# Second forward transform stage as 64x32 matmul tiles, with forward shuffles from 64 partitions to eight on two DMA queues

## The chip, the cores and the metric

One core of a Trainium2 chip runs the whole kernel. The metric is the device time in microseconds of one execution; the profile's times are microseconds from the start of its span. TensorE (PE) does the matmuls, VectorE (DVE) and ScalarE (ACT) read the results out of PSUM ("evacuation"), GpSimd (POOL) does small work and issues DMAs, SyncE (SP) issues DMAs only.

## The reference

A long convolution per channel, gated, and then an MLP over the tokens. S = 2048 tokens, D = 448 channels, F = 1792; everything that matters is this:

```python
x = A_q
h  = x + A(layernorm(x), A_k, A_v, A_shift_k, A_ssm_k, A_ssm_D)
h2 = h + B(layernorm(h), B_w1, B_b1, B_w2, B_b2)

def A(q, k, v, shift_k, ssm_k, ssm_D):
    kv = causal_shift_conv(k, shift_k) * v          # 4 taps, per channel
    y  = irfft(rfft(pad(kv, 2 * S)) * rfft(pad(ssm_k, 2 * S)))[:S]
    return q * (y + kv * ssm_D)

def B(x, w1, b1, w2, b2):                            # over the tokens
    u = gelu(einsum("bsd,sf->bdf", layernorm(x), w1) + b1)
    return transpose(einsum("bdf,fs->bds", u, w2) + b2)
```

## The kernel before

The transforms are matmuls with tables of sines that the kernel builds itself. Tokens are split as 128 partitions times R = 16, so a forward transform has two stages. The same two stages run for the filter (tag "k", source `KT`, target `TK`) and for kv (tag "u", source `V`, target `TU`).

First stage, `emit_stage1` (matmul at L1040): 128x32 tiles, four of them side by side in the columns of the array, so that 8 matmuls fill one pair of PSUM banks, 128 x 896 values. One evacuation (L1050, or L1048 where the term with `ssm_D` is added for the filter, which only DVE does) writes the pair into a buffer in SBUF. A group is four such pairs (`jh` 0 to 3); there are four groups for k and four for u, so 16 evacuations each. After `jh` 1 and after `jh` 3, half of the group's buffer is moved by three DMAs (L1056): partitions 0 to 31 and 96 to 127 by POOL, 32 rows to 8 partitions each, and 32 to 95 by SP, 64 rows to 16 partitions. Each names the columns of `TK` or `TU` that it writes, which is half of them.

Second stage, `emit_stage2` (matmul at L1075): 8 pairs `jj`, and in each pair two PSUM buffers `h`. Each buffer takes four matmuls with 128 rows and 64 columns of the block table `FW`, and is evacuated (through `evac`, L719 and L720 on ACT, L722 and L723 on DVE) over the input in `TK` or `TU`.

Then `emit_products_i1` multiplies the two spectra on DVE (L1108, 16 products), runs the first inverse stage in 64x128 tiles (L1120), evacuates, and shuffles back by POOL and SP DMAs (L1144, and L1133 for the last pair) to 8 partitions each. The second inverse stage `emit_i2` (L1240) combines, normalizes and feeds `emit_mlp` (L1365, L1375, L1387). Ahead of all this `emit_kT` transposes the filter (L1019), and `emit_kv` transposes k (L947), makes the short convolution by matmuls with 64 rows (L973), and multiplies by v on DVE (L988).

Nothing of this order is fixed in the code. `_Sched` collects all operations with their dependences, and a list scheduler places them on the engines: an engine that is free takes the ready operation with the lowest rank. The ranks are the numbers in `WHEN`, one for each step of a tag in the order in which the steps are emitted; `WHERE` says for operations that may run on ACT or DVE whether they go to ACT ("a"), to DVE ("d") or to whichever the scheduler finds ("f"). Buffers come from pools: `psum` has 8 banks, taken in pairs by the transform stages; `gring` holds the first stage's group buffers.

`emit_tables` builds `FW` for the second stage, and `MA`, `MB` and `MN` for the first inverse stage, from a per-partition index (`pc`, bit fields) and iotas on POOL.

Of the kernel before, what the change touches and what calls it, by code (L numbers as in the profile page):

```python
# [7 lines left out]
ALU = mybir.AluOpType  # L8
# [4 lines left out]
    "dummy": (283,),  # L13
    "tables": (138, 234, 288, 20, 81, 325, 139, 217,),
    "loads": (91, 107, 134, 143, 231, 216, 80, 297, 0, 238, 183, 285, 228, 299, 145,),
    "kv": (290, 148, 151, 174, 63, 282, 100, 192, 205, 47, 18, 112, 141, 45, 207, 160, 233,),
    "kT": (201, 13, 14, 175, 200, 130, 54, 53,),
    "k1": (132, 135, 152, 226, 122, 144, 165, 213, 68, 51, 154, 167, 89, 168, 262, 336,),
    "k2": (23, 150, 83, 97, 224, 227, 140, 153, 258, 248, 180, 195, 169, 219, 338, 235,),
    "u1": (71, 86, 116, 123, 46, 82, 176, 221, 117, 215, 261, 316, 173, 184, 277, 278,),  # L20
    "xload": (156, 298, 314, 302,),
    "bias": (75, 171,),
    "q": (271, 208, 318, 93, 268, 185, 279, 280, 264,),
    "u2": (133, 142, 220, 210, 241, 249, 64, 114, 159, 196, 137, 189, 1, 115, 252, 251,),
    "i1": (179, 121, 99, 3, 190, 96, 186, 149, 188, 240, 203, 202, 128, 92, 212, 95,),
    "ct": (36, 187, 87, 300,),
    "xn": (257, 17, 6, 222, 161, 317,),
    "w1a": (329, 239, 230, 55,),
    "w1b": (306,),
    "warm": (291, 307, 265, 27, 292, 147, 330, 320, 5, 304, 270, 38, 19, 315, 284, 62, 333, 327, 105, 118, 191, 295,  # L30
        324, 259, 56, 8, 332, 113, 236, 273, 206, 198, 182, 274,),
    "i2": (260, 69, 103, 39, 15, 31, 293, 28, 108, 242, 90, 84, 88, 331, 22, 197, 204, 33, 110, 237, 164, 323, 256,
        310, 73, 214, 223, 170, 44, 79, 157, 177, 16, 211, 328, 281, 131, 250, 4, 247, 158, 294, 109, 40, 29, 104,
        34, 243, 267, 129, 98, 287, 70, 178, 67, 162, 246, 120, 155, 2, 125, 11, 229, 42, 253, 272, 59, 124, 119,
        266, 12, 78, 194, 276, 127, 41, 313, 10, 102, 61, 255, 21, 37, 66, 24, 232, 199, 321, 312, 76, 308, 296, 52,
        111, 303, 163, 319, 58, 65, 339, 209, 26, 326, 337, 289, 85,),
    "w2": (146,),
    "mlp": (218, 57, 136, 126, 77, 30, 25, 48, 60, 9, 305, 72, 166, 245, 301, 172, 50, 181, 418, 419, 420, 421, 422,
# [3 lines left out]
    "kv": "ddaffffa",  # L42
    "kT": "fadfdddd",
    "k1": "fafaafaffaff",
    "k2": "dfdffadaafdafada",
    "u1": "fffaafadaaddafaa",
    "bias": "a",
    "u2": "fdaafafaaaaadafa",
    "i1": "affadfaaffdaffaf",
    "ct": "ffda",  # L50
    "xn": "aaff",
    "i2": "aaffaadafddf",
# [518 lines left out]
def _build(nc, A_q, A_k, A_v, A_shift_k, A_ssm_k, A_ssm_D, B_w1, B_b1, B_w2, B_b2, out):  # L571
# [5 lines left out]
    Bsz, S, D = A_q.shape  # L577
# [48 lines left out]
    with ctx:  # L626
# [47 lines left out]
        o_GR = (o_WR, o_WR + 8 * DB, o_X, o_X + 8 * DB)  # L674

        def GR_(s):
            return view(o_GR[s], [R // 4, 2, D])
# [13 lines left out]
        gring = _Pool(4)  # L691
# [36 lines left out]
        def emit_tables():  # L728
# [6 lines left out]
            o_p = small(80)  # L735
            frow = view(o_fr, [128], i32)
            srow = view(o_s, [16], i32)
            pc = view(o_p, [12], i32)
            pcf = view(o_p + 48, [6], f32)
# [33 lines left out]
            op("pool", lambda e, W: e.iota(pc[:, 0:1], [[0, 1]], base=0, channel_multiplier=128), w=[(o_p, 4)])  # L773
            op("pool", lambda e, W: e.iota(gcol, [[0, 8], [512, 16]], base=0, channel_multiplier=0), w=[(o_gc, 512)],
               n=128, est=190.0)
            op("pool", lambda e, W: e.iota(chi, [[0, 2], [1, 4], [0, 16]], base=0, channel_multiplier=0),
               w=[(o_gc + 512, 512)], n=128, est=190.0)
            for a, b_, c_ in ((0, 112, 14), (112, 128, 2)):
# [3 lines left out]
                op("pool", lambda e, W, a=a, b_=b_, c_=c_: e.iota(chm[:, a:b_], [[0, 2], [1, 4], [0, c_]], base=0,  # L782
                                                                 channel_multiplier=0),
                   w=[(o_gc + 2048 + 4 * NB, 512, "cm")], n=128, est=190.0)
            for k, (b0, st_) in enumerate(((2048, -2048), (2048, 2048), (0, 2048))):
                for a, b_ in (((0, 128),) if k == 0 else ((0, 112), (112, 128))):
                    op("pool", lambda e, W, k=k, b0=b0, st_=st_, a=a, b_=b_: e.iota(
                        cph[:, 128 * k + a:128 * k + b_], [[st_, 2], [0, (b_ - a) // 2]], base=b0, channel_multiplier=0),
                       w=[(o_gc + 1536 + 512 * k, 512, "cp%d" % k)], n=128, est=190.0)
# [7 lines left out]
            fields = ((5, 12), (0, 2048), (9, 3), (7, 15), (7, 15), (11, 3), (13, 1), (11, 2))  # L797
            o_fd = small(64)
            fd = view(o_fd, [16], i32)
            for i, (sh, mk) in enumerate(fields):  # L800
                op("pool", lambda e, W, i=i, sh=sh: e.memset(fd[:, i:i + 1], sh), w=[(o_fd + 4 * i, 4)], est=34.0)
                op("pool", lambda e, W, i=i, mk=mk: e.memset(fd[:, 8 + i:9 + i], mk), w=[(o_fd + 32 + 4 * i, 4)], est=34.0)
            op("dve", lambda e, W: e.tensor_tensor(out=pc[:, 4:12], in0=pc[:, 0:1].broadcast_to([128, 8]), in1=fd[:, 0:8],
                                                   op=ALU.logical_shift_right),
               r=[(o_p, 4), (o_fd, 32)], w=[(o_p + 16, 32)], n=8)
            op("dve", lambda e, W: e.tensor_tensor(out=pc[:, 4:12], in0=pc[:, 4:12], in1=fd[:, 8:16], op=ALU.bitwise_and),
               r=[(o_p + 16, 32), (o_fd + 32, 32)], w=[(o_p + 16, 32)], n=8)
            for i in (10, 11):
                op("dve", lambda e, W, i=i: e.tensor_tensor(out=pc[:, 4:5], in0=pc[:, 4:5], in1=pc[:, i:i + 1],
                                                            op=ALU.bitwise_or),  # L810
# [639 lines left out]
```

## Time and profile before

| | before |
|---|---|
| median of 3 runs | 178.2 us (177.69 to 178.92) |
| profiled execution: its own time, its span | 178.13 us, 175.9 us |
| PE, DVE, ACT, POOL busy | 166.1, 102.0, 92.2, 63.3 us |
| second stage matmuls (L1075) | 128, 15.8 us busy |
| first stage matmuls (L1040) | 256, 15.3 us busy |
| first inverse stage matmuls (L1120) | 128, 14.0 us busy |
| forward shuffles (L1056), POOL | 32 of 112 KB, median 3.8 us to landing |
| forward shuffles (L1056), SP | 16 of 224 KB, median 3.7 us to landing |
| inverse shuffles (L1144), POOL | 14 of 196 KB, median 4.6 us to landing |

A group of instructions is read as line, engine, operation, output from input, shapes, count, then busy time and mean duration of one, then the idle time of its engine just before and what ended it. A duration of a matmul is its latency; matmuls overlap, so busy time is less than count times duration. The chain of waits is followed back from the last instruction, at each step to what released it.

### The profile page before, as it was taken

To read this page: it belongs to the slowest core of one execution; us is meant where nothing else is said; L and a number is where in the kernel's file an instruction comes from. 1 tells how busy PE (TensorE), PEld (TensorE's weight loads), DVE (VectorE), ACT (ScalarE), POOL (GpSimd) and SP (SyncE) were. 2 spreads that over 40 slices of the span, in tenths; PEclk is the share of its full clock that TensorE was granted. 3 is DMA by queue.
4 is the path that set the end of the run, shared out by engine and by line. 5 is a ranking of instruction groups with operands and counts; after the bars stand their busy time and mean duration, and the time that the engine had idled before them with its cause. 6 is when DMAs were issued, how large, how long until landed. Compare 5 with 4: busy or idle time off the path is not lost.

```text
span 175.9 us, 3619 instructions
## 1 busy us (share of the span) xinstructions
PE 166.1 (94%) x1445; PEld 95.6 (54%) x1445; DVE 102.0 (58%) x189; ACT 92.2 (52%) x131; POOL 63.3 (36%) x157
## 2 busy tenths in 40 slices
PE   6999999879979999998999999999999999999994
PEld 2786745342323333644544455555557777777784
DVE  6995696848999999998998860000001231331331
ACT  3799958888979999966982656412120000000000
POOL 8576628670600643894888760000000000000000
PEclk9999999999999999999999999999999999999999
DMA  5999855992849386569999999910000111011111
GB/s 174 416 334 332 268 165 201 325 352 71 250 98 383 110 214 198 167 179 390 383 396 405 421 419 417 419 77 0 0 4 0 52 52 52 16 40 52 52 52 52
DMA packets 15444, 35.13 MB, mean 200 GB/s; under 512 B 3820, under 2 KB 9484, under 8 KB 15428
## 3 DMA queue, kind: packets, MB, share of 16 engines
q1 hardware_dynamic: 12164, 28.00, 43.4%
q0 software_dynamic: 3072, 6.80, 12.6%
q8 instruction: 11, 0.18, 0.4%
q10 hardware_dynamic: 192, 0.11, 0.2%
q14 instruction: 5, 0.04, 0.1%
HBM read 22.05 MB, written 1.84 MB: 136 GB/s over the span
## 4 chain that ended last, share of the span: by engine, by line
PE 68%; ACT 10%; POOL 7%; DMA 7%; DVE 4%; issue 2%; DVEq 0%; POOLq 0%
PE ps L1387 24%; PE ps L1375 12%; PE ps L1365 9%; ACT arena L719 8%; DMA arena<-arena 7%; PE ps L1040 4%; PE ps L1006 3%; POOL arena L1056 3%; PE ps L947 3%; PE ps L1240 3%; PE ps L1075 2%; PE ps L1019 2%; PE ps L973 2%; PE ps L1120 2%; DVE arena L1259 1%
## 5 line engine op out<-in xcount | busy, mean ns | idle before, releaser
L1390 DVE SCALAR_TENSOR_TENSOR arena<-ps,arena 128x448 bf16<-128x448 f32 (+2 forms) x17 | 11.1, 656 | 57.4 <-PE ps L1387 57.4
L1387 PE MATMUL ps<-arena 128*128 128x448 bf16 (+2 forms) x238 | 42.7, 342 | 0.0
L1387 PEld LDWEIGHTS ps<-arena 128*128 128x128 bf16 x238 | 33.3, 145 | 9.5
L719 ACT CAST arena<-ps 128x896 bf16<-128x896 f32 (+1 forms) x29 | 23.4, 948 | 1.2 <-PE ps L1075 1.1
L1365 PE MATMUL ps<-arena 128*128 128x448 bf16 x112 | 22.9, 353 | 0.4 <-DVE arena L1318 0.4
L1056 POOL DMA_DIRECT2D arena<-arena x32 | 17.5, 553 | 14.1 <-ACT arena L1050 12.9
L1050 ACT CAST arena<-ps 128x896 bf16<-128x896 f32 x24 | 20.3, 919 | 3.8 <-PE ps L1040 3.5
L1375 PE MATMUL ps<-arena 128*128 128x448 bf16 x112 | 21.8, 353 | 0.0
L1075 PE MATMUL ps<-arena 128*64 128x448 bf16 x128 | 15.8, 360 | 3.4 <-DMA arena<-arena 1.8
L1355 ACT ACTIVATE arena<-ps,arena 128x448 bf16<-128x448 f32 x14 | 8.6, 633 | 19.4 <-PE ps L1375 17.7
L1108 DVE TENSOR_TENSOR arena<-arena 128x1792 bf16<-128x1792 bf16 x16 | 16.7, 1080 | 0.2
L1365 PEld LDWEIGHTS ps<-arena 128*128 128x128 bf16 x112 | 10.6, 98 | 11.5 <-DVE arena L1318 2.5
L1375 PEld LDWEIGHTS ps<-arena 128*128 128x128 bf16 x112 | 10.9, 98 | 10.2
L1040 PE MATMUL ps<-arena 128*32 128x448 bf16 x256 | 15.3, 356 | 0.4 <-DVE arena L988 0.3
L1120 PE MATMUL ps<-arena 64*128 64x448 bf16 x128 | 14.0, 352 | 1.0 <-ACT arena L719 0.9
L1144 POOL DMA_DIRECT2D arena<-arena x14 | 8.2, 588 | 17.4 <-ACT arena L719 16.6
L1075 PEld LDWEIGHTS ps<-arena 128*64 128x64 f16 x128 | 5.7, 108 | 12.8 <-ACT arena L719 3.6
L1287 ACT ACTIVATE arena<-arena 128x448 bf16<-128x448 f32 x14 | 8.0, 575 | 5.9 <-DVE arena L1259 5.7
L988 DVE TENSOR_TENSOR arena<-ps,arena 128x512 bf16<-128x512 f32 (+1 forms) x16 | 9.0, 617 | 2.7 <-PE ps L973 2.7
L1120 PEld LDWEIGHTS ps<-arena 64*128 64x128 f16 x128 | 5.1, 94 | 9.5 <-ACT arena L719 5.0
L719 ACT COPY arena<-ps 128x1024 bf16<-128x1024 bf16 (+1 forms) x9 | 8.9, 1019 | 0.9 <-PE ps L1154 0.6
L1040 PEld LDWEIGHTS ps<-arena 128*32 128x32 f16 x256 | 5.1, 95 | 7.8 <-DVE arena L988 1.9
(94 smaller groups left out, 207.0 us busy)
## 6 DMA issues: line engine op xcount, KB each, us to landing
arena<-in_B_w_dram SPq DMA_DIRECT2D x8, 896.0 KB, 12.0
arena<-in_B_w_dram SPq DMA_DIRECT2D x2, 2048.0 KB, 17.1
arena<-arena SPq DMA_DIRECT2D x16, 224.0 KB, 3.7
arena<-arena POOLq DMA_DIRECT2D x32, 112.0 KB, 3.8
arena<-in_B_w_dram SPq DMA_DIRECT2D x2, 1536.0 KB, 18.7
arena<-arena POOLq DMA_DIRECT2D x14, 196.0 KB, 4.6
arena<-in_A_k_dram SPq DMA_DIRECT2D x4, 448.0 KB, 5.7
arena<-in_A_v_dram SPq DMA_DIRECT2D x4, 448.0 KB, 9.0
```

Source lines behind the costliest of these rows:

```text
L719: return e.copy(out=dst(), in_=src())
L988: return e.tensor_tensor(out=v, in0=u.rearrange("p t (r d) -> p t r d", d=64), in1=v, op=ALU.mult)
L1040: op("pe", lambda e, W, b=b, r=r, q=q, x=x, c0=c0: e.matmul(PS[32 * q:32 * q + 32, b.slots[x], 0:D], E[:, 2 * r + x, c0:c0 + 32], src[:, r ...
L1050: return e.copy(out=dst, in_=Ppair(b)) if W == "act" else e.tensor_copy(out=dst, in_=Ppair(b))
L1056: shuf[tag].append(op(q_, lambda e, W, g=g, i=i, a=a, nu=nu, jh=jh: e.dma_start(T[a + i:a + i + 4 * nu - 3:4].rearrange("p (j k) c d -> p ...
L1075: op("pe", lambda e, W, b=bs[h], h=h, j=j, c=c, par=par: e.matmul(PS[64 * par:64 * par + 64, b.slots[c], 0:D], FW[:, 64 * c:64 * c + 64], ...
L1108: op("dve", lambda e, W, m=m, i=i: e.tensor_tensor(out=MR(m.slots[0]).rearrange("p (x y) d -> p x y d", x=2), in0=TU[:, i].unsqueeze(2).br ...
L1120: k = op("pe", lambda e, W, b=bs[h], m=ms[h], par=par, t=t, tab=tab, xy=xy, P=P: e.matmul(Pb(b, par), tab[P, :], MR(m.slots[0])[P, xy, :], ...
L1365: op("pe", lambda e, W, r=r, fc=fc, b=bs[fc]: e.matmul(Pb(b), W1A[:, r, 128 * fc:128 * fc + 128], Q[:, r, :], start=(r == 0), stop=(r == R ...
L1375: op("pe", lambda e, W, r=r, fc=fc, b=b: e.matmul(Pb(b), W1B[:, r, 128 * (fc - n0):128 * (fc - n0) + 128], Q[:, r, :], start=(r == 0), sto ...
L1387: op("pe", lambda e, W, r=r, fc=fc, b=b, d0=d0, d1=d1: e.matmul(Pb(b)[:, d0:d1], W2[fc // 7][:, fc % 7, r:S:R], G[:, fc, d0:d1], start=(fc ...
L1390: op("dve", lambda e, W, r=r, b=b, A=A, d0=d0, d1=d1: e.scalar_tensor_tensor(out=X[:, r, d0:d1], in0=Pb(b)[:, d0:d1], scalar=bm[:, r:r + 1 ...
```

## The change

The second stage's matmuls become 64x32 tiles: 16 in each pair `jj`, which cover both buffers `h`, with the two row halves of the array and its four column strips used in turn (`tile_position`). The columns are paired as `jj` and `jj + 8` in place of `2 jj` and `2 jj + 1`; products, first inverse stage and inverse shuffles follow this pairing.

The first stage's groups are halved: eight groups of two pairs for k and eight for u, with the four 32-column tiles of one pair taken from two rows `r` in place of four. Eight buffers of half the size hold them. When a group is complete, two DMAs move it, rows 0 to 63 by POOL and rows 64 to 127 by SP, each to 8 partitions, 224 KB; for the upper half the target's two blocks of 32 partitions are exchanged. Each names all of `TK` or `TU` as its target.

The tables change to match (one more bit field, an exclusive or, other iota patterns), the row with `ssm_D` is loaded twice, and `WHEN` and `WHERE` hold new numbers for all tags ahead of the MLP's last matmuls.

```diff
 WHEN = {
...
-    "kv": (290, 148, 151, 174, 63, 282, 100, 192, 205, 47, 18, 112, 141, 45, 207, 160, 233,),
+    "kv": (133, 102, 131, 266, 43, 156, 243, 35, 101, 150, 178, 236, 261, 245, 244, 210, 230,),
...
-    "k1": (132, 135, 152, 226, 122, 144, 165, 213, 68, 51, 154, 167, 89, 168, 262, 336,),
-    "k2": (23, 150, 83, 97, 224, 227, 140, 153, 258, 248, 180, 195, 169, 219, 338, 235,),
-    "u1": (71, 86, 116, 123, 46, 82, 176, 221, 117, 215, 261, 316, 173, 184, 277, 278,),
+    "k1": (145, 213, 62, 134, 116, 139, 68, 198, 99, 158, 0, 160, 183, 196, 231, 246,),
+    "k2": (40, 27, 212, 26, 93, 137, 141, 185, 163, 215, 57, 138, 220, 79, 305, 6,),
+    "u1": (228, 254, 197, 232, 47, 238, 182, 250, 45, 87, 49, 154, 168, 284, 95, 214,),
...
-    "u2": (133, 142, 220, 210, 241, 249, 64, 114, 159, 196, 137, 189, 1, 115, 252, 251,),
-    "i1": (179, 121, 99, 3, 190, 96, 186, 149, 188, 240, 203, 202, 128, 92, 212, 95,),
+    "u2": (37, 5, 157, 165, 132, 294, 179, 201, 151, 34, 162, 277, 229, 82, 268, 314,),
+    "i1": (226, 56, 108, 105, 135, 115, 64, 202, 65, 58, 199, 200, 28, 83, 123, 143,),
...
-        o_GR = (o_WR, o_WR + 8 * DB, o_X, o_X + 8 * DB)
+        o_GR = tuple(o + 4 * DB * s for o in (o_WR, o_X) for s in range(4))
...
-        gring = _Pool(4)
+        gring = _Pool(8)
...
-            fields = ((5, 12), (0, 2048), (9, 3), (7, 15), (7, 15), (11, 3), (13, 1), (11, 2))
+            fields = ((7, 6), (0, 2048), (10, 1), (8, 15), (8, 15), (12, 3), (12, 1), (10, 8), (11, 8))
...
-            for i in range(R // 4):
+            for i in range(R // 2):
                 g = _Buf(gring)
-                for jh in range(4):
+                pi = 32 * (i >> 2) + (i & 3)
+                for jh in range(2):
...
-                    if jh % 2 == 0:
-                        continue
-                    for q_, a, nu in (("pool", 0, 8), ("pool", 96, 8), ("sp", 32, 16)):
-                        shuf[tag].append(op(q_, lambda e, W, g=g, i=i, a=a, nu=nu, jh=jh: e.dma_start(
...
-                           br=[g], w=[(o_T + (4 * j + jh - 1) * 2 * DB, 4 * DB, tag) for j in range(4)],
-                           dmab=4 * nu * 4 * DB, keng=nu, rate=350.0))
+                for t in range(2):
+                    p0 = 64 * t + (pi ^ 32 * t)
+                    shuf[tag].append(op("sp" if t else "pool", lambda e, W, g=g, p0=p0, t=t: e.dma_start(
+                        T[p0:p0 + 29:4].rearrange("p (j k) c d -> p j (k c d)", k=2),
+                        GR_(g.slots[0])[64 * t:64 * t + 64].rearrange("p k c d -> p (k c d)")),
+                       br=[g], w=[(o_T, 32 * DB, tag)], dmab=64 * 4 * DB, keng=8, rate=350.0))
...
-                for h in range(2):
-                    sch.t0 = (T_K2 if scale else T_U2) + T_D2 * (2 * jj + h)
-                    for c in range(2):
-                        for par in range(2):
-                            j = 2 * jj + par
-                            op("pe", lambda e, W, b=bs[h], h=h, j=j, c=c, par=par: e.matmul(
-                                PS[64 * par:64 * par + 64, b.slots[c], 0:D], FW[:, 64 * c:64 * c + 64], T[:, j, h, :],
-                                start=True, stop=True),
+                for c in range(2):
+                    sch.t0 = (T_K2 if scale else T_U2) + T_D2 * (2 * jj + c)
+                    for h in range(2):
+                        for F_ in range(2):
+                            for t in range(2):
+                                j = jj + 8 * F_
+                                g0 = 64 * (t ^ h) + 32 * F_
+                                P = slice(64 * t, 64 * t + 64)
+                                op("pe", lambda e, W, b=bs[h], h=h, j=j, c=c, g0=g0, P=P, t=t: e.matmul(
+                                    PS[g0:g0 + 32, b.slots[c], 0:D], FW[P, 32 * c:32 * c + 32], T[P, j, h, :],
+                                    start=True, stop=True, tile_position=(64 * t, g0)),
...
```

## The prediction

> **What bounds the kernel now.** I read the page first, then busy time by stretch, then the chain of waits, then the timeline around the two places where a forward stage hands its data to the next. The page gives the frame:
>
> ```profile
> span 175.9 us, 3619 instructions
> PE 166.1 (94%) x1445; PEld 95.6 (54%) x1445; DVE 102.0 (58%) x189; ACT 92.2 (52%) x131; POOL 63.3 (36%) x157
> PE 68%; ACT 10%; POOL 7%; DMA 7%; DVE 4%; issue 2%; DVEq 0%; POOLq 0%
> ```
>
> A busy share of 94% for TensorE is an average over very different stretches, and TensorE's ends are modelled. The stretches tell more (start and end, length, then busy time and number of instructions for PE, PEld, DVE, ACT, POOL):
>
> ```profile
> 18.00:36.00 18.00, 16.29 (x358) 9.11 (x356) 14.10 (x21) 14.53 (x18) 10.60 (x21) 1.00 0.75 244
> 36.00:52.00 16.00, 14.74 (x168) 5.97 (x168) 13.30 (x14) 13.41 (x17) 5.67 (x11) 1.00 0.59 188
> 52.00:73.00 21.00, 19.16 (x186) 7.63 (x184) 20.59 (x27) 20.73 (x26) 8.24 (x15) 1.00 0.68 212
> 92.00:175.90 83.90, 81.01 (x439) 52.34 (x437) 21.37 (x44) 14.97 (x30) 10.63 (x27) 1.00 0.35 137
> ```
>
> From 92 us on it is the MLP's matmuls, which the change doesn't touch. From 52 to 73 us (second stage of u, products, first inverse stage) DVE and ACT are both busy 98 to 99% of the time: nothing that TensorE does faster shows there. From 36 to 52 us DVE is idle for 16.00 - 13.30 = 2.70 us and ACT for 2.59 us, some 2.6 us each. The number of evacuations is the same after the change (16 a stage, 896 columns each), so 2.6 us is the most that this stretch can give back. The clock column is 1.00 throughout, so clock plays no part.
>
> The chain of waits shows what that idle time is made of (start, length, what):
>
> ```profile
> 28.25 1.53 POOL arena L1056 x3
> 29.85 1.03 POOL arena L1056 x2
> 30.93 4.97 DMA arena<-arena
> 35.99 0.96 PE ps L1075 x8
> 37.95 0.95 PE ps L1075 x8
> 39.67 0.97 PE ps L1075 x8
> ...
> 45.70 1.07 POOL arena L1056 x2
> 46.77 4.02 DMA arena<-arena
> 50.83 0.99 PE ps L1075 x8
> ```
>
> Twice it runs through forward shuffles: POOL issues them (L1056), they land, and only then does the second stage (L1075) run, for k at 35.99 and for u at 50.83. The matmuls of the second stage stand in it too, four times for about 0.96 us and, at 63.42, once for 0.51.
>
> **The change, part by part.** All sums are against the profiled execution: span 175.9, its own time 178.13 us, that is 2.2 us around the span. It lies 0.07 below the median of 178.2, which I neglect.
>
> (1) **Second stage on TensorE.** Removed: 128 matmuls of 128x64 tiles (8 for each of 16 pairs). Added: 256 of 64x32 tiles, 16 a pair. In the timeline four old ones take 0.57 us and eight 0.95: 95 ns for each further one and 0.19 of lead and tail. No row shows eight tiles side by side. Bound from below: the first stage's 128x32 tiles, four side by side, take 0.94 us for 16, so (0.94 - 0.19)/16 = 47 ns; eight side by side would need 23.5, and a pair 16 x 0.0235 + 0.19 = 0.57. Bound from above: no better than those four, 0.94, no gain. The row nearest in shape is the kv stage (64-row tiles, a weight load for each, 64 to 256 columns): 108 in 3.68 us, 34 ns apart although short, which gives 16 x 0.034 + 0.19 = 0.73. I take the middle of 0.57 and 0.73, 0.65: 0.30 less a pair, 4.8 us of busy time over 16 pairs. On the path are the four pieces of 0.96: **-1.2 us** (ends: -1.6 and 0). The half piece gains nothing, since both evacuations of a pair now wait for the last of 16 matmuls, where one could start after four (0.57). The two PSUM pairs are also taken together; the evacuations queued behind them are ACT's and DVE's, which from 52 us on have work in stock all the time, so I cost this at nothing; without that stock it is 0.08 for each of 8 pairs, 0.6 us.
>
> The row for a floor is the kv stage's 34 ns. [...]
>
> (2) **Issues of the forward shuffles.** The group rows:
>
> ```profile
> L1056 POOL DMA_DIRECT2D arena<-arena x32 | 17.5, 553 | 14.1 <-ACT arena L1050 12.9
> L1075 PE MATMUL ps<-arena 128*64 128x448 bf16 x128 | 15.8, 360 | 3.4 <-DMA arena<-arena 1.8
> ```
>
> The last line above is to be read with its idle column: 3.4 us in which TensorE stood before a second-stage matmul, 1.8 of it for shuffles. POOL's issues go from 32 to 16 (17.5 us to 16 x 0.55 = 9), SP's stay 16. SP's old ones took 537 ns, and the inverse shuffles to 8 partitions take 672 on SP and 587 on POOL; I take these two. At the end of u's first stage the last evacuation ends at 44.81 and POOL's last issue at 46.77, 1.96 later, because two issues for each half group are queued. With one on POOL beside one on SP that is about 0.3 + 0.6 = 0.9: **-1.05** there. At k's end five issues in a row (28.25 to 30.89, 2.6 us) become two or three; what that is worth is in (4).
>
> (3) **Landing.** Old: 112 KB to 8 partitions from POOL 3.8 us, 224 KB to 16 partitions from SP 3.7 (medians). New: 224 KB to 8 partitions from both; no row shows it. Nearest: POOL's inverse shuffles, 196 KB to 8 partitions, 4.6 us median, 5.5 at most. On the line through 112 and 196 KB, 28 KB more adds 0.3: 4.9 us, **+1.2** for whatever waits for a landing (ends: 0, if bytes and not partitions decide, and +1.8). At u's end, (2) and (3) make +0.15.
>
> [...]
>
> (4) **Order and what may start.** The old shuffles left after each half of a group and named half of the second stage's input; k's second stage began at 35.99 on its first half, while k's last first-stage evacuation ran until 35.55 (DVE, L1048). Now every shuffle names all of the input: the second stage waits for all sixteen. Against that the priority table changes: the kv stage's matmul steps go from ranks 18 to 233 to ranks 150 to 261, and k's first stage from 51 to 336 down to 0 to 246. So k's first stage comes ahead of much of kv (7.5 us of matmuls in the timeline) and of u, and its landing lies under them. Then the wait at 35.9 is gone: DVE stood 1.40 us and ACT 0.73 there, mean **-1.07**. If this cover fails, see the second rival.
>
> (5) **Nearly free.** The tables get two memsets (98 ns), one small DVE operation (144) and slower iotas (by L776, 0.70 against 0.32 for the flat one), in all some 1 us of POOL before 8.2 us, where POOL stands 2.02 idle; the second stage's table is made by 15.1 and first read at 35.99. Without this cover: 1 us. One more load of D on SP is 0.43 us, in a queue that is empty from 10.1 to 16.5. Two k evacuations fewer must run on DVE (1082 against 919 on ACT). Inverse shuffles keep count and size. The later stages' ranks change too; from 52 to 73 us both evacuating engines are full, so 0; half a us either way.
>
> **Sum:** -1.2 - 1.05 + 1.2 - 1.07 = -2.1, within the 2.6 that the stretch holds: 178.13 - 2.1 = **176.0 us**. With (1) and (3) at their ends: 175.5 (held by the 2.6) to 177.8.
>
> **Rivals.** *Gain off the path.* Eight tiles run no faster than four, or TensorE just waits longer: (1) is 0 and (3) stays, 178.13 - 0.9 = 177.2; if kv merely takes the place of the covered wait, 178.3. For it: PEld waits on ACT L719 for 5.0 us before L1120 and on L719 and L720 for 6.2 us before L1075, so TensorE is often the one that waits. Against it: DVE L723 waits 2.3 us and ACT 2.2 for L1075.
>
> *The whole-input wait, slower.* At u's end 0.9 + 4.9 = 5.8 us pass from the last evacuation to the first second-stage matmul. Before, eight k evacuations (44.88 to 48.9) and four of u's first half (48.9 to 50.8) filled it; the latter can't now. It decides if fewer than about twelve k evacuations (half a us each on two engines) are left then; with eight, 5.8 - 4.0 = 1.8 us are bare. At k's end, if its last evacuation still comes at 35.55, landing is 41.35, 5.3 later than 35.99, and u's six remaining evacuations fill 3: 2.3 bare. Both, less 1.2 from (1): +2.9, **181.0**. For it: in the old order halves were what kept both engines at work. Against: k's stage moved ahead in the ranks.
>
> *The order fills more.* DVE and ACT idle 3.9 and 3.5 us from 18 to 36 too; if k's early evacuations use 1.5 of that beyond the ceiling of 175.5: 174.0.
>
> **How the numbers follow.** Forecast 0.44, gain off the path 0.18, whole-input wait 0.30, order fills more 0.08. The time is the first's, 176.0, its own range 175.5 to 177.8. The range reaches from 174.0 to 181.0, which leaves out little at the bottom and the worst third of the slower case. A measurement of this kernel can tell about 1%, 176.4 and 180.0. Over 1% faster: three quarters or more of the forecast and all of the last, with a little of the second, 0.46; within 1%: the rest of these and the mildest of the slower case, 0.26; slower 0.28.
>
> **What would show it.** Right: the stage-two groups of 16 in 0.6 to 0.7 us, POOL's shuffle issues x16 at about 0.59, landings near 4.9, k's first stage finished before 31 us, and MLP matmuls starting about 2 us earlier than 92.46. Wrong: groups of 16 at 0.9 us; a second-stage matmul that waits for a landing with ACT and DVE both idle for over 1.5 us; or ACT busy less than 20 of the 21 us in the product stage.

## The result, and the profile after

| | before | after |
|---|---|---|
| median | 178.3 us (177.69 to 178.92) | 192.55 us (191.62 to 193.22) |
| ratio to before | | 1.0795 [1.0736, 1.0855] |
| profiled span | 175.9 us | 190.6 us |
| first forward shuffle issued, last one landed | 16.5, 50.8 us | 20.8, 62.5 us |
| first MLP matmul starts (L1365, after L1370) | 85.6 us | 99.5 us |

The change costs 14.2 us, and 13.9 of them have been lost before the MLP begins. Line numbers move: the first stage's evacuation is now L1055, the shuffle L1060, the second stage's matmul L1080.

The page after, first the frame (busy time, share of the span, instructions) and the shares of the chain of waits:

```profile
span 190.6 us, 3847 instructions
PE 166.0 (87%) x1573; PEld 94.6 (50%) x1573; DVE 102.2 (54%) x189; ACT 92.7 (49%) x132; POOL 53.4 (28%) x143
PE 65%; DMA 13%; ACT 11%; DVE 4%; POOL 4%; issue 2%; DVEq 0%; POOLq 0%; ACTq 0%
```

No compute engine has more to do than before: PE 166.0 for 166.1, DVE 102.2 for 102.0, ACT 92.7 for 92.2. Only the span has grown, and DMA's share of the chain has gone from 7 to 13%. So most of the loss is waiting. The chain of waits (start, length, what) tells for what:

```profile
21.70 0.93 ACT arena L1055 x2
22.63 13.01 DMA arena<-arena
...
36.67 1.52 PE ps L976 x24
...
43.21 5.41 DMA arena<-arena
48.63 0.14 issue
48.76 0.89 PE ps L1080 x25
...
56.47 6.01 DMA arena<-arena
62.48 0.04 issue
62.52 1.35 PE ps L1080 x23
```

24.4 us of the chain are forward shuffles. The first 13.01 are not the second stage's wait, but the first stage's: a group buffer comes free only when both of its shuffles have landed, all eight are taken, and ACT (L1055) stands until one has been emptied. The other two are the second stage of k and of u. The row for the shuffles, and the groups of what waits for them (busy, mean ns | idle before, releaser):

```profile
L1060 SPq DMA_DIRECT2D arena<-arena x16: 613/1820/3824, 20.8 to 56.5; - x16
L1060 POOL DMA_DIRECT2D arena<-arena x16: 562/564/826, 21.1 to 49.5; - x16
DMA to landing us min/median/max: 5.4/9.2/11.8
```

```profile
L1055 ACT CAST arena<-ps 128x896 bf16<-128x896 f32 x24 | 20.4, 910 | 13.1 <-DMA arena<-arena 6.5
L1080 PE MATMUL ps<-arena 64*32 64x448 bf16 x256 | 13.6, 446 | 9.1 <-DMA arena<-arena 6.2
L1060 POOL DMA_DIRECT2D arena<-arena x16 | 9.3, 584 | 18.9 <-ACT arena L1055 16.0
```

A landing of a POOL shuffle takes 9.2 us in the median, where before it took 3.8 (the profile gives no landings for SP's shuffles here; the 13.01 us of the chain are one of them). An issue on SP takes 1.8 us in place of 0.54; the profile doesn't say why. Busy time by stretch (PE, PEld, DVE, ACT, POOL, then granted clock, DMA's busy share, GB/s) shows that this isn't a longer latency, but a slower flow:

```profile
24.00:28.00 4.00, 3.73 (x88) 2.16 (x84) 3.21 (x6) 1.87 (x3) 1.71 (x4) 1.00 0.95 213
28.00:32.00 4.00, 2.10 (x48) 1.23 (x52) 1.01 (x3) 2.62 (x3) 0.56 (x1) 1.00 0.97 191
32.00:36.00 4.00, 0.88 (x20) 0.36 (x16) 1.29 (x2) 0.30 (x1) 0.56 (x1) 0.97 0.92 212
36.00:40.00 4.00, 2.33 (x40) 1.97 (x42) 1.02 (x2) 2.32 (x3) 0.00 (x0) 0.50 0.62 207
```

The DMA engines are 92 to 97% busy and move only 191 to 213 GB/s. In the kernel before, 30 to 34 us had 0.94 and 276 GB/s, 34 to 38 us 0.94 and 370. ACT works 0.30 us of the four from 32 to 36, DVE 1.29. The last row shows a second loss that follows: behind four us in which PE was busy for 0.88, its granted clock is 0.50. Over the whole run the granted clock is 0.955, where before it was 1.000. By an estimate from these two and the span of 190.6 us that is about 17 us at half clock, between 36 and 67 us, and it comes up again in (1) below.

### The profile page after: what moved, and what is told of

It is laid out like the page before. It is cut to its first block, busy times and chain, and to the rows that moved or that the text cites. A ratio compares the mean times of both kernels' runs of the same rounds, so it can differ in the third digit from the quotient of the medians.

```text
span 190.6 us, 3847 instructions
## 1 busy us (share of the span) xinstructions
PE 166.0 (87%) x1573; PEld 94.6 (50%) x1573; DVE 102.2 (54%) x189; ACT 92.7 (49%) x132; POOL 53.4 (28%) x143
## 4 chain that ended last, share of the span: by engine, by line
PE 65%; DMA 13%; ACT 11%; DVE 4%; POOL 4%; issue 2%; DVEq 0%; POOLq 0%; ACTq 0%
PE ps L1392 22%; DMA arena<-arena 13%; PE ps L1380 11%; PE ps L1370 9%; ACT arena L719 8%; PE ps L1080 4%; PE ps L1125 3%; PE ps L1159 3%; PE ps L1045 3%; PE ps L1245 2%; PE ps L976 2%; PE ps L1022 2%; PE ps L950 2%; ACT arena L1055 2%; ACT arena L720 1%
## 5 line engine op out<-in xcount | busy, mean ns | idle before, releaser
L719 ACT CAST arena<-ps 128x896 bf16<-128x896 f32 x28 | 23.0, 967 | 8.2 <-PE ps L1080 6.0
L1055 ACT CAST arena<-ps 128x896 bf16<-128x896 f32 x24 | 20.4, 910 | 13.1 <-DMA arena<-arena 6.5
L1370 PE MATMUL ps<-arena 128*128 128x448 bf16 x112 | 22.7, 353 | 0.5 <-DVE arena L1323 0.5
L1080 PE MATMUL ps<-arena 64*32 64x448 bf16 x256 | 13.6, 446 | 9.1 <-DMA arena<-arena 6.2
L1380 PE MATMUL ps<-arena 128*128 128x448 bf16 x112 | 21.5, 352 | 0.0
L1113 DVE TENSOR_TENSOR arena<-arena 128x1792 bf16<-128x1792 bf16 x16 | 16.5, 1084 | 0.5 <-ACT arena L719 0.3
L1370 PEld LDWEIGHTS ps<-arena 128*128 128x128 bf16 x112 | 10.7, 98 | 11.4 <-DVE arena L1323 1.9
L1149 POOL DMA_DIRECT2D arena<-arena x14 | 8.2, 588 | 28.9 <-ACT arena L719 28.7
L1060 POOL DMA_DIRECT2D arena<-arena x16 | 9.3, 584 | 18.9 <-ACT arena L1055 16.0
L976 PE MATMUL ps<-arena 64*128 64x128 bf16 (+3 forms) x208 | 9.2, 244 | 4.8 <-ACT arena L1055 4.8
L1080 PEld LDWEIGHTS ps<-arena 64*32 64x32 f16 x256 | 3.7, 99 | 18.7 <-DMA arena<-arena 5.6
L976 PEld LDWEIGHTS ps<-arena 64*128 64x128 bf16 x208 | 7.5, 105 | 8.4 <-ACT arena L1055 5.5
L719 ACT COPY arena<-ps 128x1024 bf16<-128x1024 bf16 (+2 forms) x9 | 8.5, 969 | 4.7 <-PE ps L1022 4.6
```

Of the source, the lines that this page charges most:

```text
L719: return e.copy(out=dst(), in_=src())
L976: op("pe", lambda e, W, b=b, i=i, cc=cc, t=t, dl=dl, i0=i0, i1=i1, rs=rs, sh=sh, o=o, P=P, m=m, one=one: e.matmul(PS[:, b.slots[t], o:o + ...
L1055: return e.copy(out=dst, in_=Ppair(b)) if W == "act" else e.tensor_copy(out=dst, in_=Ppair(b))
L1060: shuf[tag].append(op("sp" if t else "pool", lambda e, W, g=g, p0=p0, t=t: e.dma_start(T[p0:p0 + 29:4].rearrange("p (j k) c d -> p j (k c ...
L1080: op("pe", lambda e, W, b=bs[h], h=h, j=j, c=c, g0=g0, P=P, t=t: e.matmul(PS[g0:g0 + 32, b.slots[c], 0:D], FW[P, 32 * c:32 * c + 32], T[P, ...
L1113: op("dve", lambda e, W, m=m, i=i: e.tensor_tensor(out=MR(m.slots[0]).rearrange("p (x y) d -> p x y d", x=2), in0=TU[:, i].unsqueeze(2).br ...
```

## Experiments: is it the flow of the shuffles?

Every forward shuffle moves the same 7.34 MB in all kernels below. Three readings are compared: the time; when the last forward shuffle landed; and the rate, which is added up from the packet records over the time in which both queues have shuffles open (for a kernel that uses one queue, that queue). Before: 304 GB/s (POOL 139, SP 165). After: 188 (POOL 105, SP 83). The rate depends on what is called open: counted only where packets of both queues are in flight it is 308 before and 203 after, so differences of less than a tenth between two rates say little. A time without an interval is from one or two runs and says nothing about differences of a per cent.

The expectations call their theories by letters. All are conjectures; no record names the engine of a packet. A1: SP's transfers to 8 partitions run on the same eight DMA engines, POOL's on all sixteen by turns. A2: POOL's run on SP's eight too. A alone is what A1 and A2 share: the number of target partitions sets the number of engines. B: the writing into few partitions is the limit, whichever engine does it. D: POOL's partitions choose its engines. E: transfers in flight together get in each other's way when they all lie in one half of the partitions. The 400 GB/s of some ranges is an estimate, about twice the rate of after (203 by the second count).

**poolboth: all shuffles from POOL.** PE, DVE and ACT keep the order of after.

```diff
-                    shuf[tag].append(op("sp" if t else "pool", lambda e, W, g=g, p0=p0, t=t: e.dma_start(
+                    shuf[tag].append(op("pool", lambda e, W, g=g, p0=p0, t=t: e.dma_start(
```

> Both 64-row shuffles of a group from POOL, none from SP; the order on PE, DVE and ACT is that of the changed kernel to the letter. Theory A1 (an SP transfer into 8 partitions always runs on the same eight DMA engines, and POOL's take turns over all sixteen): some 400 GB/s while shuffles run, landings near 4.5 us, 177 to 182 us. Theory A2 (POOL's transfers run on the same eight as SP's, too): still about 205 GB/s, landings near 9 us, 190 to 195 us. Theory B (the limit is the writing into few partitions, whichever engine does it): as A2.

Measured: 181.5 us, ratio 1.0181 [1.0133, 1.0228], 259 to 265 GB/s. The row of the shuffles, and by stretch:

```profile
L1060 POOL DMA_DIRECT2D arena<-arena x32: 562/562/826, 23.1 to 48.7; - x32
DMA to landing us min/median/max: 4.0/5.8/7.6
```

```profile
28.00:32.00 4.00, 3.07 (x72) 1.63 (x64) 3.02 (x5) 1.29 (x2) 1.80 (x4) 1.00 1.03 306
32.00:36.00 4.00, 2.73 (x64) 1.75 (x66) 1.54 (x3) 3.44 (x5) 3.62 (x7) 1.00 0.94 248
```

At the same busy share of DMA the rate is 248 to 306, landings come in 5.8 us, and 11 of the 14 us are back, although POOL now issues 32 shuffles and SP none. Eight target partitions on their own are therefore not what costs the 14 us, and theory B and A2 as they were worded, with 190 to 195, fall; A1 has the time but not its 400 GB/s. The tiles, the order and the whole-input wait are all still there too. Together with the 32 issues on POOL they leave 3.2 us, net of whatever this kernel gains.

**spboth: all from SP** (the same line with `"sp"`; the scheduler's order changes).

> Both 64-row shuffles of a group from SP, none from POOL. Theory A: every one of them on the same eight engines, 7.34 MB at 205 GB/s, 36 us from the first to the last landing: 190 to 200 us. If it is instead the mixing of POOL's and SP's packets on one engine that costs time, SP alone is as fast as POOL alone was, 180 to 183 us.

Measured: 206.8 us, above the range of theory A, 175 to 179 GB/s. SP by itself has in the records 8 packets in flight, each 3584 bytes in 140 ns.

**sp4: SP's half cut in two.** 32 rows to 4 partitions each, in place of 64 to 8. The instructions of PE, DVE and ACT come line by line as in after.

> SP's 64-row shuffle cut into two of 32 rows into 4 partitions each; POOL's as in the changed kernel. Theory A: an SP transfer then has only four engines, about 100 GB/s alone and less beside POOL; SP's 3.67 MB take some 40 us or more, 200 to 215 us in all. Theory B: the same eight partitions are written at a time, so 190 to 195 us.

Measured: 203.9 us; SP by itself moves 97 to 101 GB/s with 4 packets in flight. SP's semaphores go the same way: a transfer to 16 partitions comes in as 16 steps (before), one to 8 as one early step and 8, one to 4 as one early step and 4. Half the target partitions, half the packets in flight (4 for 8) and little more than half the rate (97 to 101 GB/s for 175 to 179): on SP the packets in flight go with the number of target partitions. That each of them is a DMA engine at work is the author's reading.

**fr_b8: the kernel before, with SP's 64 rows to 16 partitions issued as two DMAs of 32 rows to 8.** One step of the plan issues both, so that the order is that of before.

```diff
-                        ... e.dma_start(T[a + i:a + i + 4 * nu - 3:4]..., GR_(g.slots[0])[a:a + 4 * nu, ...]),
+                        ... [e.dma_start(T[b + i:b + i + 29:4]..., GR_(g.slots[0])[b:b + 32, ...])
+                             for b in range(a, a + 4 * nu, 32)],
```

> The kernel before with its order kept on every engine; only SP's DMA of 64 rows to 16 partitions is issued as two of 32 rows to 8 partitions, one after the other. Theory D: SP's bytes then lie on the eight engines that also carry POOL's rows 0 to 31; these eight move 5.5 of 7.34 MB, at 205 GB/s 27 us and more, 183 to 192 us. Theory B (partitions): the same partitions are written, 178 to 180 us.

Measured, in one run: 185.5 us against 179.1 for the kernel before beside it, 6.4 more, with nothing else of the change in it but 16 further issues on SP, whose own price isn't told apart; 218 GB/s (POOL 113, SP 105), last landing at 58.2 us. **b_sp8**, the same cut without keeping the order, is of no use: the scheduler made another plan, and its 200.2 us mix both.

> The kernel before, with SP's 64 rows to 16 partitions cut into two DMAs of 32 rows to 8 partitions, both on SP. Theory A2 (all transfers into 8 partitions share the same eight engines): 7.34 MB at about 205 GB/s, 36 us, 188 to 194 us. Theory A1 (POOL takes turns over sixteen): the lower eight carry 5.5 MB, 27 us, 180 to 184 us. Theory B: no change, 178 to 179 us, and 16 more SP issues.

## Experiments: why do two queues carry less than one?

In after, SP and POOL, each to 8 partitions a transfer, together move 188 GB/s, less than POOL alone in poolboth (259 to 265).

**swap: lower half from SP, upper from POOL**, order kept.

> The changed kernel with the two queues exchanged: rows 0 to 63 of a group (into the lower 64 partitions) go from SP, rows 64 to 127 (into the upper 64) from POOL. The same DMAs, the same order on every engine, only the issuer of each half changes. Theory D (a POOL transfer runs on engines that its partitions choose, the lower half on the eight that SP always uses, the upper half on the other eight; so in the changed kernel both queues sat on the same eight, and POOL alone with both halves had sixteen): now the queues don't meet, about 400 GB/s, landings under 5 us, 177 to 182 us. Theory A2 (POOL's run on SP's eight whatever they move) and theory B (few partitions are the limit): as the changed kernel, 191 to 195 us.

Measured: 192.0 us, ratio 1.0732 [1.0691, 1.0774], 194 GB/s. By that it doesn't matter which half is whose (192.55 in after). The idea that POOL's engines follow its partitions (theory D) falls.

**noflip: without the exchange of the 32-partition blocks** in the upper half (`p0 = 64 * t + pi`), order kept.

> The changed kernel without the exchange of the 32-partition blocks in the upper half: target p0 = 64 t + pi for both halves, and one exclusive or less in the table. Order and DMAs are otherwise the same. Theory D and theory A2: the block within a half doesn't choose the engines, 190 to 195 us. [...]

Measured: 195.4 us, 191 GB/s. The exchange doesn't cause the loss; by this one run after is, if anything, 2 to 3 us better with it.

**turn_lo and turn_hi: small extra DMAs on POOL**, 15 between the shuffles or 16 with one ahead of the first, in case POOL's transfers take two sets of engines by turns, as A1 supposes. PE, DVE, ACT and SP keep the order of after, line by line.

> The changed kernel with a tiny DMA of 8 rows of 16 bytes issued by POOL between each two of its shuffles (15 in all), into bytes that nothing reads; otherwise the order of every engine is kept. If POOL's transfers take eight engines in turn, each shuffle now comes on the same turn as the first. Theory A1: that is the turn that SP's eight engines are on, all shuffles share eight engines, landings 9 us and more, 193 to 205 us. Theory A2 (POOL's always run on SP's eight anyway) and theory B: as the changed kernel, 191 to 195 us.

> The same with one more tiny DMA, ahead of POOL's first shuffle: 16 in all. Nothing else differs between the two kernels. Theory A1: each of POOL's shuffles comes on the other turn, on the eight engines that SP doesn't use; the two queues run side by side at about 400 GB/s, landings under 5 us, 178 to 184 us, at least 10 us below the kernel with 15. Theory A2 and theory B: the same time as with 15 tiny DMAs, within 1 us.

Measured: 190.0 and 194.3 us with 15, 190.75 and 193.2 with 16. Theory A1 asked for at least 10 us between them; two runs each show no difference. Taking turns in this sense isn't shown.

**one16 and mend16: 16 target partitions for each DMA, as in SP's old ones.** one16 moves a whole group of 128 rows in one DMA to 16 partitions 8 apart, from POOL and SP by turns. mend16 gives a group four rows `r` of one half, moved to 16 partitions 4 apart in that half, the lower by POOL, the upper by SP. Both keep the eight tiles; the order changes.

```diff
+                        T[i:i + 121:8].rearrange("p (j k) c d -> p j (k c d)", k=2),       # one16
+                        T[p0:p0 + 61:4].rearrange("p (j k) c d -> p j (k c d)", k=2),      # mend16, p0 = 64 * t + (i >> 1)
```

> One DMA for all 128 rows of a group, into 16 partitions at a distance of 8, POOL and SP by turns; the second stage's table is built for this order of rows. Same bytes, same row size, same matmuls. Theory A (A1 and A2, the number of engines is set by the 8 target partitions): sixteen engines, about 400 GB/s, landings of 448 KB under 5 us, no evacuation that waits for a buffer, 175 to 180 us. Theory B (writes into few partitions are the limit; as many partitions are written at a time as in the changed kernel): about 205 GB/s and 188 to 194 us.

> Eight 64x32 tiles as in the changed kernel, but a first-stage group is four rows r of one half, so that one DMA of 128 rows goes to 16 partitions 4 apart within that half, POOL for the lower half and SP for the upper; the table follows. Theory A (the engines set the limit, and 16 partitions give sixteen): landings of 448 KB in 3 to 5 us, no wait for a group buffer, 176 to 181 us; what is then left against the kernel before is the order, the whole-input wait and the tiles. If the target's spacing is what counts (the run with partitions 8 apart was at 205 GB/s with all sixteen), then about 400 GB/s only while both halves are written at once, 178 to 185 us.

Measured: 203.0 us, ratio 1.1397 [1.1343, 1.1451], 220 GB/s; and 193.4 us, ratio 1.0875 [1.0812, 1.0938], 247 GB/s. Sixteen target partitions were not enough, and none of the ranges expected holds (175 to 180 or 188 to 194; 176 to 181 or 178 to 185). The packet records show more: 16 packets are in flight, but each takes longer. Medians of POOL's 7168 bytes and SP's 3584 bytes, from 20 to 62 us, are in this table with the other kernels:

```
             POOL ns  (upper quartile)   SP ns  (upper quartile)   GB/s, queues open
before        276          394            140        142              304
after         360          864            140        141              188
poolboth      274          440              -          -              259
one16         541          560            279        287              220
mend16        449          525            204        261              247
```

In the author's reading there are two effects: how many engines a transfer may use (SP has 8 packets in flight in spboth, 4 in sp4), and whether its packets get in each other's way at the partitions (POOL's take 449 ns in mend16 for 274 in poolboth). In after they would meet: with both queues open 10.0 packets of POOL and 3.6 of SP are in flight in the mean, their sum seldom above 17, while SP alone, in spboth, has about 8. This fits POOL's packets holding engines on which SP's would run; no record shows it. The last four runs are meant to separate the two.

**alt: the queues change halves from group to group.** Order, bytes, partitions and instructions of after.

```diff
-                    shuf[tag].append(op("sp" if t else "pool", ...
+                    shuf[tag].append(op("sp" if t ^ (i & 1) else "pool", ...
```

> Only the queue of each shuffle is changed: of one group POOL moves the lower half and SP the upper, of the next the other way round. Instructions, their order on every engine, partitions and bytes are those of the changed kernel. Theory E, halves: the transfers that one queue has in flight together must not all lie in one half of the partitions. In the changed kernel the records show 13 or 14 packets of POOL in flight beside 3 of SP, and a packet of POOL takes 360 ns in the median and 864 in the upper quartile, where the same packets take 274 and 440 when POOL's transfers go to both halves by turns (all 32 on POOL, 181.5 us). With the queues changing halves POOL's two transfers in flight lie in different halves, so POOL's packets go back to about 275 and 450 ns, both queues together move 250 to 300 GB/s in place of 188 to 205, and the time is 181 to 184 us. Theory A2, engines: SP's transfers to 8 partitions always sit on the same 8 of 16 engines, and three quarters of all bytes on half of the engines give about 0.67 of the 304 GB/s of before, 203 GB/s, whichever half a queue moves; then nothing changes here: 191 to 193 us. [...]

Measured: 190.7 us, ratio 1.0676 [1.0598, 1.0753]. POOL's packets did get shorter (273 ns in the median, 525 in the upper quartile) and the rate rose to 213, but the time hardly followed: some 2 us, and its interval overlaps that of after. The row shows who is late:

```profile
L1060 SPq DMA_DIRECT2D arena<-arena x16: 613/1720/2862, 20.8 to 51.4; - x16
L1060 POOL DMA_DIRECT2D arena<-arena x16: 562/564/826, 21.1 to 45.6; - x16
```

POOL issues its last shuffle at 45.6 us, 3.9 earlier than in after; SP's last goes out at 51.4 and lands at 60.7, and the second stage needs both. SP's share of the bytes, in transfers to 8 partitions, sets the end. Theory E's median was right, its rate (250 to 300) and its time were not, the time by almost 7 us; theory A2's 191 to 193 is missed by 0.3.

**p3: SP moves only every second upper half**, a quarter of the bytes; order on PE, DVE and ACT kept.

```diff
+                    shuf[tag].append(op("sp" if t and i & 1 else "pool", ...
```

> The changed kernel with SP moving only the upper half of every second group, 8 transfers, and POOL the other 24. Only POOL's and SP's lists change. Theory E: POOL's transfers lie in both halves, SP's in one; near the kernel with all 32 on POOL but with fewer issues in a row: 180 to 183 us. Theory A2: SP's share on its 8 engines is a quarter of the bytes, so these engines carry 0.62 of all bytes in place of 0.75: 304 x 0.5 / 0.62 = 245 GB/s, less than the 259 to 265 of POOL alone: 182 to 186 us.

Measured: 186.6 us, ratio 1.0438 [1.0348, 1.0529]. With half, a quarter and none of the bytes on SP the time is 192.55, 186.6 and 181.5: 5 to 6 us for each quarter. It lies above theory E's range and 0.6 above that of A2.

**b_port: the kernel before, the three partition ranges moved.** Sizes, target partitions (8, 8, 16), queues and order of before; POOL now has the lower half, SP the upper.

```diff
-                    for q_, a, nu in (("pool", 0, 8), ("pool", 96, 8), ("sp", 32, 16)):
+                    for q_, a, nu in (("pool", 0, 8), ("pool", 32, 8), ("sp", 64, 16)):
```

> The kernel before, in which only the partition ranges of the three shuffles are moved: POOL takes 0 to 31 and 32 to 63, SP 64 to 127, where POOL took 0 to 31 and 96 to 127 and SP 32 to 95. Sizes, the number of target partitions (8, 8, 16), queues and the order on every engine are those of before. Theory E: now POOL's transfers all lie in the lower half and SP's in the upper, as in the changed kernel; the rate falls from 304 GB/s to 200 to 250, and the time rises by 4 to 8 us, to 182 to 187. Theory A2: the engines are the same as before, so nothing changes: 178 to 179 us.

Measured: 181.5 us, ratio 1.0157 [1.0087, 1.0227], 251 GB/s. SP's packets go from 140 to 156 ns (upper quartile 142 to 231), POOL's from 276 to 345. Where partitions alone move, the kernel gets slower by about 3 us (1.6 to 4.1 by the interval): less than E's 4 to 8, and against A2's nothing.

```profile
L1056 POOL DMA_DIRECT2D arena<-arena x32: 544/544/811, 16.5 to 49.8; - x32
L1056 SPq DMA_DIRECT2D arena<-arena x16: 532/553/1202, 16.2 to 48.4; - x16
DMA to landing us min/median/max: 3.0/5.1/7.4
```

The median landing is 5.1 in place of 3.7 us. Why the place of the partitions matters isn't shown, and theory E doesn't cover one16, whose 16 target partitions lie 8 apart in both halves: it measured 220 GB/s.

**mend16a: mend16 with the queues changing halves from pair to pair** (POOL's issues shift a little against its small operations).

> The kernel whose groups are four rows of one half, moved in one transfer of 128 rows to 16 partitions of that half, with the queues changing halves from pair to pair (before, POOL always moved to the lower half and SP to the upper: 193.4 us, 247 GB/s). Theory E, if it is the queue's transfers in flight together that collide: packets of POOL fall from 449 ns in the median to under 400, and the time to 185 to 190 us. If it is the 16 packets of one transfer that collide among themselves in one half, nothing changes: 193 us. Theory A2 has all 16 engines in both: 193 us.

Measured: 194.1 us, 231 GB/s, no better. There the 16 target partitions of a single transfer already lie in one half; changing the queue can't spread them.

Now the kernels that keep the order of before or of after, sorted by the last landing (us; the fourth column is what the profiled run still takes after it, its own time less the last landing):

```
            first issue   last landing   profiled run   still to come   median time
before          16.5          50.8           178.1          127.3          178.3
b_port          16.2          54.1           181.0          126.9          181.5
fr_b8           17.7          58.2           185.5          127.3          185.5

poolboth        23.1          53.4           183.7          130.3          181.5
p3              20.7          57.2           187.2          130.0          186.6
alt             20.8          60.7           191.6          130.9          190.7
turn_hi         22.2          62.2           193.2          131.0          192.0
after           20.8          62.5           192.4          129.9          192.55
swap            22.1          63.1           193.1          130.0          192.0
turn_lo         22.2          64.1           194.3          130.2          192.1
noflip          22.8          65.2           195.4          130.2          195.4
sp4             22.3          74.0           203.9          129.9          203.9
```

What is still to come differs by no more than 0.5 us in the first group and 1.2 in the second, while the last landing moves by 7 and by 21 us. So within one order the last landing of the shuffles sets the time (poolboth, whose second stage of u starts 1.9 us after its last landing, fits the row but not the reason). Against before, after has lost 11.7 us at the last landing and 2.6 behind it.

The 11.7 us aren't all flow. The stretch from first issue to last landing has grown from 34.3 to 41.7 us, by 7.4; the other 4.3 are a first shuffle that goes out later, ahead of any other. That belongs to the new order: seven of k's evacuations have ended by then (20.7 us), where before the third one (16.4 us) released it. poolboth starts later still, has 30.3 us from first issue to last landing, and so ends almost with before: at its 259 to 265 GB/s the late start does no harm.

What the two parts cost by themselves in the kernel before, 6.4 us for SP's eight target partitions (fr_b8, one run) and 3.1 for the halves (b_port), makes 9.5 of the 14.2; in the changed kernel they aren't additive, since curing the halves alone (alt) gives 2 us back and taking SP away 11. None of the kernels was faster than the one before.

## Why the prediction was wrong, step by step

The prediction was 176.0 us, range 174.0 to 181.0. The measured 192.55 lies outside.

**(1) Tiles: right, and better than taken.** The timeline of after has whole groups of 16:

```profile
78.44 0.59 PE L1080 MATMUL ps<-arena 64*32 64x448 bf16 x16
...
80.87 0.57 PE L1080 MATMUL ps<-arena 64*32 64x448 bf16 x16
```

0.57 us is the lower bound worked out from 23.5 ns a matmul; 0.65 was taken. But the stage's busy time fell by 2.2 us (15.8 to 13.6) and not by 4.8, in part for a reason that the prediction had put aside ("clock plays no part"). Two groups at a granted clock of 1.00, and two while it is 0.50 (until 66.5 us):

```profile
48.76 1.03 PE L1080 MATMUL ps<-arena 64*32 64x448 bf16 x32 [1.04 <-DMA arena<-arena]
64.82 1.93 PE L1080 MATMUL ps<-arena 64*32 64x448 bf16 x32 [0.58 <-ACT arena L719]
```

On the chain of waits the second stage's matmuls have grown from 4.4 to 6.7 us, so nothing of the gain shows there: the stage waits for landings, and part of it runs at half clock.

**(2) Issues: right for POOL, wrong for SP.** POOL's 16 took 584 ns in the mean, as taken (587). SP's 672 ns became 1820 in the median. What a longer issue alone costs isn't shown.

**(3) Landing: the step that failed.** The text put the new landing at 4.9 us and let it cost 1.2 us, at most 1.8. It read a landing as the latency of one transfer, on a line through 112 and 196 KB. What bounds it is a rate: 7.34 MB at 188 instead of 304 GB/s take 39.0 in place of 24.1 us. That this difference, 14.9 us, is so near the whole loss is luck: by the other count of the rate (203 and 308) it is 12, and measured from first issue to last landing the stretch grew by 7.4, the rest being the late start and the 2.6 us behind. Still each is several times the 1.2 us that the sum allowed. The median landing of 9.2 us fits waiting behind other shuffles, as the same 224 KB from POOL land in 5.8 in poolboth. The text priced the landing for one transfer, and not for all 16 of SP in a row, which go to 8 partitions each where they went to 16 (9 semaphore steps for 16), next to POOL's. A row in the trace warned of it: before, the stretch from 18 to 22 us had DMA at 0.89 busy, that from 34 to 38 at 0.94. The DMA engines were nearly full in the stage that was changed, and there half of SP's target partitions went.

**(4) Order: not what happened.** k's first stage was to come ahead and its landings were to lie under other work. Instead the evacuations of the first stage stood for buffers (ACT L1055 waits 6.5 us for DMA), and PE's second stage of k began at 48.76, 12.8 us after the 35.99 of before. The first shuffle itself had gone out 4.3 us later, behind k's seventh evacuation and not its third, so k's first stage came early but its landings did not. The half us "either way" for later stages, and full evacuating engines in the product stage, held: ACT 20.35 and DVE 20.48 of 21 us from 66 to 87 us:

```profile
66.00:87.00 21.00, 18.70 (x214) 6.23 (x206) 20.48 (x25) 20.35 (x25) 8.08 (x14) 0.99 0.58 183
```

**(5) Nearly free:** no row of after shows anything that waits for the tables, and no run priced them alone.

**The rivals.** The whole-input wait (181.0) had the right place: the second stage of u starts at 62.52 on a landing, with DVE idle for 5.31 and ACT for 5.49 us. It was named as the sign that the forecast is wrong. Its size was not right, for it used the same 4.9 us landing. Its own share lies in the 2.6 us that after loses behind the last landing. Before, four evacuations of u's first half, about half a us each on two engines, were done by then, so an estimate from them is 2 us; but the clock of 0.50 from 59.7 to 66.5 us falls on the same stretch, and no run separates the two.

## What stays open

That both queues use the same engines while SP is held to eight is the author's reading of the packets in flight (10.0 of POOL and 3.6 of SP in after, 8 of SP in spboth) and of the three points on SP's share; the records don't name the engine of a packet, so which ones either queue takes isn't shown. Nor is it shown whether packets collide where rows are read or where they are written: b_port changes both, and one16 and mend16 read all 128 rows in each transfer, which points to the written side without showing it. What half clock alone costs is open too: the chain of after has some 9 us of matmuls at 0.50, so by an estimate up to half of that, but waits may have hidden it.

## To carry to other kernels

Price a moved shuffle by rate first and by latency second: bytes of the whole stage over what its queues carry, and look at DMA's busy share in that stretch before you count a landing. For SP, count the target partitions: with 16, 8 and 4 of them it had 16, 8 and 4 packets in flight here (before, spboth, sp4), and with 8 and 4 moved 175 to 179 and 97 to 101 GB/s by itself. Spread what is in flight at one time over both halves of the partitions; b_port puts a price of about 3 us on it here. Fewer and larger DMAs were no saving in themselves (one16, with another order: half as many, 203 us).

## What the runs showed of the hardware that was not expected

- DMA's busy share didn't tell an efficient transfer from a jammed one: 0.97 at 191 GB/s (after, 28 to 32 us), 1.03 at 306 (poolboth, the same stretch).
- POOL's packets are 7168 bytes and SP's 3584 for the same kind of copy, and POOL alone to 8 partitions a transfer moves 259 to 265 GB/s where SP alone moves 175 to 179. With such transfers POOL had up to about 16 packets in flight, SP about 8.
- In two kernels a drop of the granted clock followed a stretch in which PE had little to do: 0.50 in after from 36 to 40 us, behind four us with PE busy 0.88, and 0.60 in b_port right after a stretch in which PE was busy 0.48 of 4 us.

```profile
34.00:38.00 4.00, 0.48 (x10) 0.17 (x4) 1.32 (x2) 1.71 (x2) 2.58 (x5) 1.00 1.02 254
38.00:42.00 4.00, 4.00 (x32) 2.20 (x30) 1.45 (x2) 2.77 (x4) 1.63 (x3) 0.60 1.05 266
```
